# A transformer block with conditioning on one Trainium2 core: the start of the kernel reordered under a new table of operations

## The chip, the cores and the metric

The kernel runs on one core of a Trainium2 chip. The metric is device time in microseconds (us) of one execution. The core has five engines that run their own streams of instructions and meet at semaphores: TensorE (PE; its weight loads are shown as PEld), VectorE (DVE), ScalarE (ACT), GpSimd (POOL) and SyncE (SP). SP only issues transfers here, ACT issues a few. All inputs are bf16.

## The reference

The input x has 2048 rows of 640. A conditioning vector c gives six vectors of 640: shift, scale and gate for attention, and the same for the MLP. Heads are 32 of 20 columns; a row sees itself and the 255 rows before it.

```
mod = silu(c) @ w_mod                                    # 640 -> 6 x 640: sa, ca, ga, sb, cb, gb
h = layernorm(x) * (1 + ca) + sa
q, k, v = split(h @ wqkv)                                # 32 heads of 20
p = softmax(mask(q @ k.T * 20 ** -0.5))                  # 0 <= i - j < 256
x = x + ga * ((p @ v) @ wo)
h = layernorm(x) * (1 + cb) + sb
out = x + gb * ((sigmoid(h @ w_gate) * (h @ w_up)) @ w_down)   # inner width 1536
```

## The kernel before, in words

**Tiling.** The rows are cut into eight chunks of 256 (two blocks of 128). For each chunk: layer norm (`ln1`), projections to q, k and v (`qkv`), attention in two bursts of four head groups (`attention`), output projection (`outproj`), second layer norm, and the MLP (`mlp`). Chunks overlap: the projections of chunks two ahead and the MLP of an earlier chunk fill PE while ACT does the exponentials of attention.

**How the order is made.** The code records operations (`Prog.op`: engine, function, planned duration, what it reads and writes), and `Prog.schedule` goes through the long list `PLAN` (line 353). Each number is 5 times the number of an operation plus that of its engine (0 PE, 1 ACT, 2 DVE, 3 POOL, 4 SP); the list therefore fixes the order on every engine, and which engine does an operation that several can do. `schedule` also computes planned times from the planned durations, the planned landing of each DMA (`dlat` and work in us) and instruction fetches (`FETCH`), with least start times (`tmin`). They decide which buffer of a pool a tile gets; `emit` writes the instructions and the semaphore waits, and there is no waiting for a time on the chip. An engine does its instructions in this order: one that waits holds all behind it. The list itself was found by a search outside the file that uses the planned durations.

**The start.** SP issues x's block 0, then five tiles of w_mod for shift and scale of attention (320 KB each, into the buffer of w_down, hence the name `wd`), then halves of wq and wk with blocks 2 and 3 of x between them, then wv. ACT issues c and x's block 1. On the engines:

- The conditioning chain. A product with the identity turns c into a column (line 644, PE); DVE halves it (`c_col`, line 646); ACT takes tanh (line 647); DVE makes SiLU (`siluc`, line 648) and copies it to 64 columns (`silubc`, line 651, by DVE or ACT as PLAN says). Then ten products for each of the five tiles of w_mod (`fnA`, line 679 with `S<-silubc,wd`), and DVE copies the result to `mA` (line 759).
- The norm of chunk 0, block by block (`ln_stats`): two statistics of 320 columns each and an aggregate on DVE (lines 774 and 776); an addition and a power on POOL (lines 781 and 783), which give the reciprocal deviation; the normalisation on DVE (line 796). Five products with the identity transpose a block (`pe_transposes`, `M<-ident,x`), ACT and DVE empty the banks (lines 895 and 896), and `modulate` applies scale and shift to 128x128 pieces (lines 812 and 813). The projections need these pieces and wq.
- Warm-up products. DVE zeroes a strip of the buffer `E`; six operations `warm` (line 660) multiply it, five with two products of 512 columns and one with one, 11 in all. `fill` (line 671) adds single such products: one after each conditioning tile but the last, and two after the first block's transposes, where PLAN puts them. Their results aren't used.

**Later.** Queries and keys of chunks 0 and 1 are transposed on PE; from chunk 2 on, the normalised rows (`hT`), queries and keys (`QT`, `KT`, from the four buffers `stg`) and the input of the MLP (`h2T`) are transposed by DMA (`transp_dma`, line 803), issued on SP among all other transfers. The gate vectors are written to memory (`gate<-grow`) and read back for all partitions (`gbc<-gate`); DVE, or POOL, multiplies wo and w_down by them (lines 1316 and 1253). w_down, w_gate and w_up come in parts of 384 to 576 KB over the first 85 us. Results of PE go to four banks (`M`) and one large tile (`S`, scores). A bank is free again when DVE or ACT has emptied it.

**Edge sets.** In each of 14 half-chunks beyond the first, `edge_set` makes 64 products of 64x64 (line 680, `S<-QT,KT 20*64`) for the corners of the window; its planned duration is 0.36 us before.

Of the kernel before, what the change touches and what calls it, by code (L numbers as in the profile page):

```python
# [348 lines left out]
def c_pe(n):  # L349
# [147 lines left out]
def build(nc, A_x, A_wqkv, A_wo, B_x, B_w_gate, B_w_up, B_w_down, c, w_mod, out, S=2048):  # L497
    NCH = S // CH
    P = Prog(nc)
    A = P.op  # L500
# [32 lines left out]
    p_x1 = sbpool("x1", 6, [128, D])  # L533
# [23 lines left out]
    def R(name):  # L557
        return Res(name)
# [104 lines left out]
    for i in range(6):  # L663
        o = A("pe", warm if i < 5 else lambda e, g: warm(e, g, 1), 1.03 if i < 5 else 0.52, prio=90, reads=[R_z], extra=wprev, tag="warm", writes=[R("w")])
        wprev = [o]
# [705 lines left out]
```

## Time and profile before

| what | us |
|---|---|
| median of 3 runs (326.62 to 328.47) | 326.9 |
| the profiled execution | 330.35 |
| its span, first to last instruction | 328.6 |
| first projection product on PE | 12.76 |
| PE busy | 320.4 |

A row of the profile names the line, the engine, the operation, and output and inputs by the program's names; `xN` counts instructions. In a timeline the first two numbers are start and length in us. Matmuls are pipelined, so the length of a group holds the drain of its last product; the time to the next group's start is what the group costs. A row of waits reads: engine, output and line that waited `<-` who ended the wait: us in total, times, longest. DMA rows of the chain give the issue and the time until the landing that something waited for. The granted clock is a share of PE's full clock.

### The profile page before, as it was taken

How to read it: one execution, taken by the hardware profiler on the slowest of the kernel's cores; microseconds unless marked ns; L12 is line 12 of the kernel's file. 1: busy time of each engine (PE TensorE's matmuls, PEld its weight loads, DVE VectorE, ACT ScalarE, POOL GpSimd, SP SyncE). 2: the span in 40 equal slices, each digit the busy share in tenths (PEclk: the TensorE clock that was granted, in tenths of full speed). 3: DMA queues.
4: the chain of work that ended last, by engine and by line, in shares of the span. 5: the costliest groups of instructions: out<-in, count | busy, mean ns of one | idle time of the engine just before them, and what ended most of it. 6: DMA issues, size and time to landing. Idle time of an engine off the chain costs nothing.

```text
span 328.6 us, 11961 instructions
## 1 busy us (share of the span) xinstructions
PE 320.4 (97%) x5045; PEld 239.7 (73%) x5045; DVE 204.5 (62%) x421; ACT 212.8 (65%) x229; POOL 187.6 (57%) x325
## 2 busy tenths in 40 slices
PE   5999999989999999999999999999999999999996
PEld 2666766666777777776777778777888777887885
DVE  4589878549776666874476637463846366745422
ACT  1589999586977667877586767585686667220220
POOL 3148777564967767867675665748572859201000
PEclk9899999999999999999999999999999999999999
DMA  7996989999763562424553211374030213122201
GB/s 246 372 323 167 308 167 218 161 150 349 207 92 70 115 142 67 94 63 108 128 77 60 56 25 28 61 119 119 16 90 19 65 42 77 28 60 41 82 0 42
DMA packets 73007, 38.20 MB, mean 116 GB/s; under 512 B 46586, under 2 KB 71674, under 8 KB 72954
## 3 DMA queue, kind: packets, MB, share of 16 engines
q1 hardware_dynamic: 71936, 36.29, 46.7%
q10 hardware_dynamic: 1018, 1.15, 1.1%
q8 instruction: 40, 0.66, 0.8%
q14 instruction: 13, 0.11, 0.1%
HBM read 21.30 MB, written 5.25 MB: 81 GB/s over the span
## 4 chain that ended last, share of the span: by engine, by line
PE 89%; DMA 7%; DVE 2%; issue 1%; ACT 1%; SPq 0%; ACTq 0%; DVEq 0%
PE M L679 73%; PE S L680 8%; PE M L680 6%; DMA QT<-stg 2%; DMA hT<-x 2%; DMA gbc<-gate 2%; DMA x<-in_A_x_dram 1%; PE S L679 1%; ACT E L1016 1%; PE S L671 1%; SPq L803 0%; DVE V L896 0%; DVE wd L1253 0%; DVE st L774 0%; DVE T L1136 0%
## 5 line engine op out<-in xcount | busy, mean ns | idle before, releaser
L1051 POOL TENSOR_SCALAR_AFFINE_SELECT E<-E 128x512 bf16<-128x512 bf16 x224 | 141.8, 664 | 63.7 <-PE S L680 23.5
L1042 ACT ACTIVATE E<-S 128x2048 bf16<-128x2048 f32 x56 | 105.0, 1875 | 35.4 <-PE S L680 34.2
L679 PE MATMUL M<-h2T,wu 128*128 128x256 bf16 x480 | 70.5, 273 | 0.5 <-DVE T L1136 0.5
L679 PE MATMUL M<-h2T,wg 128*128 128x256 bf16 x480 | 65.6, 273 | 0.0
L679 PE MATMUL M<-wd,hh 128*128 128x320 bf16 (+2 forms) x396 | 56.9, 295 | 0.0
L679 PEld LDWEIGHTS M<-h2T,wu 128*128 128x128 bf16 x480 | 44.8, 98 | 9.1 <-DVE T L1136 0.8
L679 PEld LDWEIGHTS M<-h2T,wg 128*128 128x128 bf16 x480 | 46.0, 98 | 6.7
L1270 ACT ACTIVATE sig<-M 128x512 f32<-128x512 f32 x48 | 28.2, 596 | 32.1 <-PE M L679 31.0
L1272 DVE SCALAR_TENSOR_TENSOR hh<-sig,M 128x512 bf16<-128x512 f32 x48 | 32.2, 678 | 26.6 <-ACT sig L1270 17.4
L679 PEld LDWEIGHTS M<-wd,hh 128*128 128x128 bf16 x396 | 37.3, 98 | 14.0
L1291 DVE TENSOR_TENSOR x<-M,x 128x320 bf16<-128x320 f32 (+2 forms) x33 | 15.5, 480 | 35.4 <-PE M L679 35.1
L680 PE MATMUL S<-QT,KT 20*64 20x64 bf16 (+4 forms) x1856 | 34.9, 211 | 0.1
L680 PEld LDWEIGHTS S<-QT,KT 20*128 20x128 bf16 (+1 forms) x1856 | 22.1, 98 | 17.6 <-issue 9.2
L1016 ACT ACTIVATE E<-S 128x2048 bf16<-128x2048 f32 x14 | 26.3, 1877 | 10.2 <-PE S L680 10.2
L774 DVE BATCH_NORM_STATS2 st<-x 128x6 f32<-128x320 bf16 x64 | 28.6, 478 | 3.5 <-DMA x<-in_A_x_dram 3.2
L1136 DVE STREAM_TRANSPOSE T<-M 128x512 f32<-128x512 f32 x32 | 21.6, 700 | 14.5 <-PE S L680 13.5
L679 PE MATMUL M<-wk,hT 128*128 128x320 bf16 x160 | 26.6, 299 | 1.1 <-DVE V L896 1.1
L679 PE MATMUL M<-wq,hT 128*128 128x320 bf16 x160 | 26.9, 299 | 0.6 <-DMA QT<-stg 0.5
L679 PE MATMUL M<-wv,hT 128*128 128x320 bf16 x160 | 27.2, 300 | 0.0
L679 PE MATMUL M<-wo,oT 128*128 128x320 bf16 x160 | 25.4, 299 | 0.0
L680 PE MATMUL M<-E,V 128*32 128x256 bf16 (+1 forms) x960 | 23.0, 246 | 0.1
L680 PEld LDWEIGHTS M<-E,V 128*32 128x32 bf16 x960 | 19.1, 97 | 4.3 <-issue 2.7
(82 smaller groups left out, 321.5 us busy)
## 6 DMA issues: line engine op xcount, KB each, us to landing
x<-in_A_x_dram SPq DMA_DIRECT2D x23, 160.0 KB, 3.7
doc<-On SPq DMA_DIRECT2D x64, 40.0 KB
wd<-in_w_mod_dram SPq DMA_DIRECT2D x6, 320.0 KB
wd<-in_B_w_down_dram SPq DMA_DIRECT2D x4, 480.0 KB
out_dram<-x SPq DMA_DIRECT2D x11, 160.0 KB, 2.1
wu<-in_w_mod_dram SPq DMA_DIRECT2D x5, 320.0 KB, 6.7
oT<-doc SPq DMA_DIRECT2D x8, 192.0 KB, 2.7
wg<-in_B_w_gate_dram SPq DMA_DIRECT2D x2, 576.0 KB
```

What stands on the lines that cost most here:

```text
L671: ins = e.matmul(p_S.aps[0][:, 3, :], Eall[:, 0:128], Eall[:, 128:640], start=True, stop=True)
L679: return e.matmul(o, l, r, start=st, stop=sp, skip_group_check=True)
L680: return e.matmul(o, l, r, start=st, stop=sp, tile_position=tp, skip_group_check=True)
L774: A("dve", lambda e, g, bi=bi, j=j: e.bn_stats(v(bi * 12 + j * 6, 6), src[bi].ap[:, j * 320:(j + 1) * 320]), 0.48, reads=[src[bi].r()], wr ...
L1016: A("act", lambda e, eng: e.activation(G.ap[:], Sp.ap[:], ACT.Exp, scale=SM_SCALE), 1.876, reads=[Sp.r()], writes=[G.r()], prio=3, tag=f"e ...
L1042: A("act", lambda e, eng: e.activation(wide()[:, :, 64:320], Sp.ap[:].rearrange("p j (t c) -> p (j t) c", c=256), ACT.Exp, scale=SM_SCALE) ...
L1051: A("pool", lambda e, eng, ap=ap, inp=inp, pat=pat, base=base, cm=cm: e.affine_select(ap(), inp(), pattern=pat, compare_op=ALU.is_ge, fill ...
L1136: A("dve", lambda e, g, h=h: e.transpose(T1.ap[:, 512 * h:512 * h + 512], X[h].ap), 0.694, reads=[X[h].r()], writes=[T1.r(h)], prio=3.5, t ...
L1270: A("act", lambda e, g, pg=pg, sg=sg: e.activation(sg.ap[:], pg.ap[:], ACT.Tanh, scale=0.5), c_act(512), reads=[pg.r()], writes=[sg.r()], ...
L1272: A("dve", lambda e, g, pu=pu, sg=sg, f0=f0: e.scalar_tensor_tensor(out=hh.ap[:, f0:f0 + 2, :], in0=sg.ap[:].rearrange("p (a b) -> p a b", ...
L1291: A("dve", lambda e, g, ps=ps, bi=bi, c0=c0, n=n: e.tensor_tensor(x1[bi].ap[:, c0:c0 + n], ps.ap[:, 0:n], x1[bi].ap[:, c0:c0 + n], op=ALU. ...
```

## The change

The table PLAN is new throughout, and so is the order on all engines. Beside it:

- Nine warm-up operations (17 products) instead of six (11). In the new table they stand thus on PE: two products, the start of the conditioning sum, two products, the product for c, ten products, transposes of block 0, two conditioning tiles, three products, the third tile, transposes of block 1, the last two tiles, and then all six fills. Before, transposes of block 0, two tiles, two fills, transposes of block 1, three tiles, four fills.
- DVE now does `c_col` between the two statistics of block 0, then aggregate, `siluc` and the normalisation of block 0, and then the statistics of block 1. Before: statistics of block 0, `c_col`, aggregate, statistics and aggregate of block 1, `siluc`, `silubc`, normalisation of block 0. `silubc` is on ACT now. Two memsets of `stg` moved from POOL to the start of DVE.
- SP issues both halves of wq one after the other (before, block 2 of x stood between them). Around 45 to 80 us, before: a part of w_down, QT, KT, KT, QT, hT, a part of w_down, hT, QT, KT, QT, KT, gbc, h2T twice. Now: QT, KT, the gate, a part of w_down, QT, KT, gbc, hT, hT, QT, a part of w_down, KT, QT, KT, h2T twice.
- The modulation of that hT, three pieces on ACT and two on DVE, is now four on ACT and one on POOL. Other evacuations and modulations of chunks 2 to 7 also moved between ACT, DVE and POOL.
- Planned figures: landing of x's block 1 (4.6 instead of 2.95 us) and of the first w_mod tiles (4.0 instead of 2.89), least start of the projections' weights 2.4, an instruction fetch left out, warm-up lengths, and 0.54 instead of 0.36 us for an edge set.

```diff
@@ -473 +474 @@ FETCH
-    4.30, 15.19, 23.69, 31.86, 36.07, 43.09, 49.13, 56.81, 65.53, 72.11, 81.79, 85.91, 94.33, 102.58, 109.61, 119.26,
+    -5, 15.19, 23.69, 31.86, 36.07, 43.09, 49.13, 56.81, 65.53, 72.11, 81.79, 85.91, 94.33, 102.58, 109.61, 119.26,
@@ load_x
-            dlat=2.95 if pool is p_x1 and b < 4 else 2.24)
+            dlat=(2.95, 4.6, 2.95, 2.95)[b] if pool is p_x1 and b < 4 else 2.24)
@@ load_w3
-                    (2.2 if hi - lo == 640 else 1.12), writes=[R_w3[k][lo // 320]] if halves else R_w3[k], prio=prio, tag=k)
+                    (2.2 if hi - lo == 640 else 1.12), writes=[R_w3[k][lo // 320]] if halves else R_w3[k], prio=prio, tag=k,
+                tmin=2.4)
...
-    load_bulk(wm_ap[0], wm_src[:, :, 0:1280], Rm[0], 0.88, 0.2, "wm0", dlat=2.89)
+    load_bulk(wm_ap[0], wm_src[:, :, 0:1280], Rm[0], 0.88, 0.2, "wm0", dlat=4.0)
@@ warm
-    for i in range(6):
-        o = A("pe", warm if i < 5 else lambda e, g: warm(e, g, 1), 1.03 if i < 5 else 0.52, prio=90, reads=[R_z], extra=wprev, tag="warm", writes=[R("w")])
+    for i in range(9):
+        o = A("pe", warm if i < 8 else lambda e, g: warm(e, g, 1), 1.03 if i < 3 else 0.6 if i < 8 else 0.3, prio=90, reads=[R_z], extra=wprev, tag="warm", writes=[R("w")])
@@ edge_set
-        last["s"] = [with_pv(f"edge{a}", sc, 0.36, rd, [G, Sp], before, 3)]
+        last["s"] = [with_pv(f"edge{a}", sc, 0.54, rd, [G, Sp], before, 3)]
```

225 rows, old and new, of the table PLAN are left out of this document.

## The prediction

> **What bounds the kernel now.** I read the page first, then who waited for whom on TensorE (PE), the busy time by stretch, and the order of time on DVE and PE in the head.
>
> ```profile
> span 328.6 us, 11961 instructions
> ## 1 busy us (share of the span) xinstructions
> PE 320.4 (97%) x5045; PEld 239.7 (73%) x5045; DVE 204.5 (62%) x421; ACT 212.8 (65%) x229; POOL 187.6 (57%) x325
> ```
> ```profile
> PE M L679 <- DVE x L796: 2.1, 1, 2.1
> PE S L660 <- DVE E L655: 1.3, 1, 1.3
> PE M L679 <- DVE V L896: 1.1, 1, 1.1
> PE M L679 <- DMA QT<-stg: 0.5, 1, 0.5
> PE M L679 <- DVE T L1136: 0.5, 1, 0.5
> ```
> ```profile
> 4.20:7.61 3.41, 1.35 (x6) 0.39 (x4) 2.12 (x8) 0.21 (x1) 1.04 (x3) 1.00 1.00 359
> 7.61:11.02 3.41, 3.36 (x40) 2.81 (x41) 0.80 (x3) 0.86 (x2) 1.00 (x2) 0.51 1.09 357
> 0.00:8.05 8.05, 4.63 (x17) 1.75 (x18) 3.63 (x12) 1.49 (x2) 3.09 (x18) 0.98 0.73 244
> 22.00:36.00 14.00, 14.00 (x278) 9.86 (x275) 13.66 (x35) 13.14 (x16) 9.82 (x13) 1.00 0.75 222
> 80.00:320.00 240.00, 240.00 (x3838) 185.19 (x3838) 142.85 (x276) 153.52 (x150) 140.67 (x232) 1.00 0.35 77
> ```
>
> PE is idle for 8.2 us in all (328.6 minus 320.4). Five waits hold 5.5 us of it: two in the head (1.3 at the very start, 2.1 before the first transposes of x) and three, 2.1 us together, between 50 and 80 us. The stretches give, after their length, busy time on PE, weight loads, DVE, ACT and POOL, then the granted clock, the DMA share and GB/s. From 80 to 320 us PE is busy 240.00 of 240 us: there a new order can lose time, hardly win any. The head is worse than its idle time shows: PE worked 1.35 of the 3.41 us to 7.61, and the granted clock of the next 3.41 us was 0.51.
>
> ```profile
> 3.21 0.89 DVE L774 BATCH_NORM_STATS2 st<-x 128x6 f32<-128x320 bf16 x2 [1.97 <-DMA x<-in_A_x_dram]
> 4.02 0.15 DVE L646 TENSOR_SCALAR c_col<-M 128x5 bf16<-128x5 f32 x1
> 4.13 0.21 DVE L776 BATCH_NORM_AGGREGATE st<-st 128x2 f32<-128x12 f32 x1
> 5.57 0.89 DVE L774 BATCH_NORM_STATS2 st<-x 128x6 f32<-128x320 bf16 x2 [1.22 <-DMA x<-in_A_x_dram]
> 6.49 0.21 DVE L776 BATCH_NORM_AGGREGATE st<-st 128x2 f32<-128x12 f32 x1
> 6.62 0.11 DVE L648 SCALAR_TENSOR_TENSOR siluc<-cth,c_col 128x5 bf16<-128x5 f32 x1
> 6.76 0.49 DVE L651 COPY silubc<-siluc 128x320 bf16<-128x320 bf16 x1
> 7.17 0.44 DVE L796 TENSOR_SCALAR x<-x,st 128x640 bf16<-128x640 bf16 x1
> ```
> ```profile
> 3.48 2.07 PE L660 MATMUL S<-E 128*128 128x512 bf16 x7
> 7.66 0.71 PE L679 MATMUL M<-ident,x 128*128 128x128 bf16 x5 [2.11 <-DVE x L796]
> 8.17 1.27 PE L679 MATMUL S<-silubc,wd 128*128 128x64 bf16 x20
> 9.25 1.04 PE L671 MATMUL S<-E 128*128 128x512 bf16 x2
> 10.09 0.74 PE L679 MATMUL M<-ident,x 128*128 128x128 bf16 x5
> 10.62 1.26 PE L679 MATMUL S<-silubc,wd 128*128 128x64 bf16 x30
> 11.71 1.03 PE L671 MATMUL S<-E 128*128 128x512 bf16 x4
> 12.76 1.74 PE L679 MATMUL M<-wq,hT 128*128 128x320 bf16 x10
> ```
>
> These are starts and lengths, in order of time. DVE waits until 5.57 for x1's transfer (1.22 us), and behind x1's statistics stand SiLU of c, its broadcast, and the normalisation of x0 (x̂0 here). So x0, in the core since 3.21, reaches PE at 7.66; then the conditioning products run partly at half clock, and the first projection starts at 12.76. From there PE is dense but for the three waits.
>
> **The change, part by part: the head.** On DVE the changed order is: half of x0's statistics, c_col, the other half, aggregate, SiLU, x̂0, and only then x1's statistics. The broadcast goes to ACT.
>
> ```profile
> 4.43 0.24 POOL L781 TENSOR_SCALAR st<-st 128x1 f32<-128x1 f32 x1 [2.05 <-DVE st L776]
> 4.75 0.58 POOL L783 TENSOR_TENSOR st<-st,mhalf 128x1 f32<-128x1 f32 x1
> ```
> ```profile
> 1.24 2.31 SPq L574 DMA_DIRECT2D wd<-in_w_mod_dram  x5
> ```
> ```profile
> wu<-in_w_mod_dram SPq DMA_DIRECT2D x5, 320.0 KB, 6.7
> ```
>
> *x̂0:* 3.21 + 0.89 + 0.15 + 0.21 ends the aggregate near 4.45; POOL's add and power (0.24 + 0.58 and 0.1 between) end near 5.4; x̂0 takes 0.44 and is ready at 5.85, not 7.61. Tanh, SiLU and broadcast lie beside POOL's power. The broadcast on ACT isn't in the trace: between 0 and twice DVE's 0.49, I take 0.49; it would have to last past 6.5 to delay a product, so it costs nothing.
>
> *Warm-ups:* nine operations are 17 products instead of 11. One takes 0.42 at half clock (9.25 to 10.09 for two), so 0.21 at full. Ten instead of seven stand behind the c product; they start at 3.48 as now, and with three more the last one ends its turn near 5.9 to 6.1. That holds x0's transposes by 0.2 us at most, and x1 is still to come: nothing on the path. In exchange PE has no gap there, and three more fill the time between the conditioning tiles.
>
> *x1:* DVE is free at 5.85, so its statistics begin 0.3 later than 5.57 and end at 6.95 (0.89 + 0.21). Add and power, 7.9; a memset and an evacuation on DVE fit in that time. x̂1 is done at 8.4, its transposes start near 8.5 instead of 10.09 and take 0.27 (half of 10.09 to 10.62).
>
> *What is late next* is w_mod. c, x0, x1 and five tiles of 320 KB are 1.97 MB, and 244 GB/s over 8.05 us is that amount: the last byte moves at 8.05. The last tile was issued near 3.1; by the median 6.7 us to landing of the same tiles of the next part it lands at 9.8. Between 8.05 and 9.8 I take 9.35, nearer to the row that includes the landing. Its ten products take 0.27 at full clock (20 took 1.08 at half): done at 9.65. Six fills now follow instead of four, 6 x 0.21 = 1.26, and the projections start at 10.95. From the last product to the first projection now pass 1.05 us (11.71 to 12.76) with copy and modulation in them; the fills cover that. So 12.76 becomes 10.95: **-1.8 us**. wq's second half goes ahead of x2 now; 400 KB at 359 GB/s are 1.1 us, so wq lands near 10.5 and 11.6, and the second is needed 0.7 after 10.95: just in time. Bounds: -2.3 if w_mod lands with x̂1, near 8.8; -0.9 at half clock (third rival).
>
> [...]
>
> **The change: 45 to 80 us.** The new table also moves DMAs in SP's queue and shares of work between DVE, ACT and POOL. The arithmetic stays, and so does the number of changes of tile mode on PE (159 in both orders).
>
> ```profile
> 49.33 7.33 DMA QT<-stg
> 56.79 2.85 PE M L679 x20
> 59.64 6.33 DMA hT<-x
> 67.77 1.23 SPq L803
> 69.10 5.02 DMA gbc<-gate
> ```
> ```profile
> L574 SPq DMA_DIRECT2D gate<-grow x1: 632/632/632, 27.3 to 27.3; - x1
> L574 SPq DMA_DIRECT2D gbc<-gate x1: 1382/1382/1382, 33.0 to 33.0; - x1
> ```
>
> The chain of waits runs through three transfers here, and the three waits of PE hang on them. A part of w_down (480 KB) stands ahead of the first QT transpose (7.33 us from issue to landing) and the next between the two of hT (6.33); DVE modulates that hT in its order and only then empties V's banks (1.1 us on PE); gbc comes last, so the scaling of w_down holds the transposes of T (0.5). In the changed order the first QT and KT stand ahead of w_down, both hT ahead of its next part, DVE modulates no tile of that hT, and gbc is issued ahead of hT. Each cause is gone, but SP and the banks have as much to do, so something else may be late in its place. Between 0 and 2.1 us I take half: **-1.1 us**. The edge sets' length, the landing times and the least start times in the planner are figures for ordering; no instruction gets longer by them: 0. In the tail the last product (192 columns), its addition and the last store stand in the same order: 0.
>
> Sum: 330.35 (the profiled execution; its span is 328.6) - 1.8 - 1.1 = 327.45. The median of the runs is 3.45 lower, 326.9; I carry the 2.9 us over: **324.0**.
>
> **Rivals.**
> *The middle gives nothing* (waits of the same size in other places): only the head counts, 325.1. For it: an order this full leaves little room, PE is already busy 14.00 of 14 us at 22 to 36. Against: each of the three waits has a cause that the order takes away.
> *The head is used up.* From 22 to 36 us DVE is busy 13.66 and ACT 13.14 of 14 us. If they set the pace there, the earlier start ends in waits: all of 1.8 is lost, 326.9 with nothing in the middle. Against it: PE has 14.00 of 14, and their work starts earlier too.
> *Half clock again.* One execution shows how the clock's stretches lie to the kernel's start. If the one with x1's transposes and the fills is half, five transposes, ten products for each of two tiles and two fills take 0.53 + 1.08 + 0.84 from 8.5 on, to 11.0, then four fills 0.84: 11.8, -0.9 for the head, 324.9 with the middle.
> *SP held: slower.* gbc now stands ahead of hT and waits for the gate's write. The first gate was issued at 27.3, and its gbc's issue ended at 34.4, so that write took up to 7 us; beside transposes it may take QT's 7.33. The w_down part, QT and KT between them cover about 3.1 (0.6 and twice 1.23). Then SP stands 4.2 us with hT behind it, and PE has no other projections: -1.8 + 4.2, 329.3. It decides from a write of 4.9 us on (no gain left); slower by over 0.5% from 6.5.
>
> **How the numbers follow.** 0.5%, 1.6 us, is about what a measurement can tell from no change, so faster is below 325.3. Chances: forecast 0.46, middle nothing 0.22, head used up 0.11, half clock 0.08, SP held 0.13. Of these faster: 0.42, 0.12, 0, 0.06, 0, together 0.60; slower 0.13; same the rest, 0.27. The range goes from 322.0 (2.3 and 2.1 from 326.9, and 0.5 of scatter) to 328.3, halfway to the slower rival from the third case; it leaves that rival out.
>
> **What would show it.** Right: PE without a gap from 1.3 to 7 us, granted clock 1.00 from 7.6 to 11, first wq product near 11.0, no waits for V, QT and T. Wrong: a first wq product after 12, a clock near 0.5 there, gbc's issue on SP lasting several us, or idle time on PE beyond 80 us.

## The result and the profile after

The changed kernel is slower: 331.75 us median of 4 runs (331.14 to 333.11) against 326.98 for before beside it (4 runs, 326.62 to 328.47). The ratio on record is 1.0115, interval 1.0066 to 1.0164 (the quotient of the two medians is 1.0146, inside it). The forecast was 324.0, the range 322.0 to 328.3. The profiled execution of after took 331.14 us.

The page, and who waited for whom on PE (engine, output, line `<-` releaser: us, times, longest), both of after:

```profile
span 329.4 us, 11959 instructions
PE 321.6 (98%) x5051; PEld 239.3 (73%) x5051; DVE 206.9 (63%) x427; ACT 212.6 (65%) x224; POOL 189.2 (57%) x324
```
```profile
PE M L681 <- DMA KT<-stg: 1.3, 2, 0.8
PE S L662 <- DVE E L657: 1.3, 1, 1.3
PE M L681 <- DVE st L776: 1.0, 1, 1.0
PE M L682 <- ACT E L1018: 0.7, 1, 0.7
PE M L681 <- POOL hT L823: 0.5, 1, 0.5
PE M L681 <- DMA QT<-stg: 0.2, 1, 0.2
```

The wait for x̂0 in the head is gone, and so are the waits for V and T. Six others stand there (KT's line holds two), five of them between 50 and 72 us; the sixth, for POOL's hT, ends at 148.75. The head of after on PE (start, length):

```profile
3.50 4.28 PE L662 MATMUL S<-E 128*128 128x512 bf16 x10
7.62 0.44 PE L681 MATMUL M<-ident,x 128*128 128x128 bf16 x5
...
11.77 2.43 PE L681 MATMUL M<-wq,hT 128*128 128x320 bf16 x16
```
```profile
5.44 0.45 DVE L798 TENSOR_SCALAR x<-x,st 128x640 bf16<-128x640 bf16 x1 [1.00 <-POOL st L785]
```

x̂0 is ready at 5.89 (5.44 + 0.45), as forecast, but its transposes start at 7.62: ten warm-up products stand ahead of them and take 4.12 us from start to start, 0.41 each. The first projection starts at 11.77, 1.0 us earlier than in the profile of before.

That profile of before was the first thing to doubt. Its execution took 330.35 us with a median of 326.9. Another execution of the unchanged kernel (e1 below) took 326.44 us, and its trace reads otherwise:

```profile
span 324.7 us, 11960 instructions
```
```profile
PE S L660 <- DVE E L655: 1.3, 1, 1.3
PE M L679 <- DVE x L796: 0.7, 1, 0.7
PE M L679 <- ACT hT L820: 0.7, 1, 0.7
```
```profile
3.48 3.19 PE L660 MATMUL S<-E 128*128 128x512 bf16 x7
7.41 0.45 PE L679 MATMUL M<-ident,x 128*128 128x128 bf16 x5 [0.73 <-DVE x L796]
10.91 1.74 PE L679 MATMUL M<-wq,hT 128*128 128x320 bf16 x10
```

Here before starts its projections at 10.91, not 12.76; the wait for x̂0 is 0.7, not 2.1; and the waits for V, QT and T, which were to be won, don't exist. So after is to be compared with this trace. Busy time by stretch (length, then busy PE, weight loads, DVE, ACT, POOL; granted clock, DMA share, GB/s), first after, then e1:

```profile
36.00:60.00 24.00, 22.07 (x429) 14.70 (x426) 19.77 (x43) 21.21 (x24) 19.05 (x34) 1.00 1.00 208
60.00:80.00 20.00, 18.63 (x291) 13.16 (x292) 12.42 (x28) 14.09 (x22) 12.06 (x20) 1.00 1.03 229
80.00:160.00 80.00, 79.39 (x1365) 58.83 (x1363) 53.67 (x109) 60.15 (x60) 60.36 (x99) 1.00 0.50 106
```
```profile
36.00:60.00 24.00, 23.20 (x436) 16.03 (x435) 19.34 (x43) 20.30 (x28) 18.51 (x33) 1.00 0.95 212
60.00:80.00 20.00, 20.00 (x334) 14.73 (x327) 15.38 (x30) 16.43 (x21) 11.81 (x20) 1.00 1.02 251
80.00:160.00 80.00, 79.99 (x1421) 59.48 (x1419) 51.93 (x109) 58.76 (x59) 60.94 (x102) 1.00 0.52 106
```

After's PE loses 1.13 us more between 36 and 60 (23.20 - 22.07), 1.37 between 60 and 80, and 0.60 between 80 and 160, where before loses nothing. The same instruction in both, products of E and V, serves as a milestone; first after, then e1:

```profile
73.56 1.50 PE L682 MATMUL M<-E,V 128*32 128x256 bf16 x64
...
161.66 1.50 PE L682 MATMUL M<-E,V 128*32 128x256 bf16 x64
```
```profile
69.82 1.59 PE L680 MATMUL M<-E,V 128*32 128x256 bf16 x64
...
157.27 1.50 PE L680 MATMUL M<-E,V 128*32 128x256 bf16 x64
```

After is 0.86 us late at the first projection, 3.74 at 70 us, 3.66 at 140 (143.68 against 140.02), 4.39 at 157, and 4.7 at the end (329.4 - 324.7). What is lost stands between the head and 74 us (2.9) and from 140 us on (1.0). The chain of waits of after shows where the first part is lost (the end of that stretch stands here); SP's issues (start, length) of after and of e1 stand below it, with w_down's part:

```profile
67.36 4.61 DMA KT<-stg
72.11 1.52 PE M L681 x10
```
```profile
61.45 1.24 SPq L805 DMA_TRANSPOSE QT<-stg  x1
62.73 0.58 SPq L575 DMA_DIRECT2D wd<-in_B_w_down_dram  x1
...
64.84 2.42 SPq L805 DMA_TRANSPOSE QT<-stg  x1
67.36 1.25 SPq L805 DMA_TRANSPOSE KT<-stg  x1
```
```profile
59.87 1.23 SPq L803 DMA_TRANSPOSE QT<-stg  x1
...
64.04 1.24 SPq L803 DMA_TRANSPOSE KT<-stg  x1
```

The last KT transpose of chunk 3 is issued 3.3 us later than in before, lands at 71.97 (67.36 + 4.61), and PE's next products start at 72.11. In e1's chain no transfer stands between 48 and 80 us.

### The profile page after: what moved, and what is told of

Same layout as the page of the kernel before. It is cut to its first block, busy times and chain, and to the rows that moved or that the text cites. A ratio compares the mean times of both kernels' runs of the same rounds, so it can differ in the third digit from the quotient of the medians.

```text
span 329.4 us, 11959 instructions
## 1 busy us (share of the span) xinstructions
PE 321.6 (98%) x5051; PEld 239.3 (73%) x5051; DVE 206.9 (63%) x427; ACT 212.6 (65%) x224; POOL 189.2 (57%) x324
## 4 chain that ended last, share of the span: by engine, by line
PE 94%; DMA 3%; DVE 1%; ACT 1%; POOL 1%; issue 0%
PE M L681 75%; PE S L682 9%; PE M L682 7%; PE S L662 2%; DMA QT<-stg 2%; DMA KT<-stg 1%; ACT E L1018 1%; PE S L681 1%; DVE T L1138 0%; PE S L673 0%; POOL hT L823 0%; DVE st L776 0%; POOL E L1053 0%; DVE stg L898 0%; DVE x L1293 0%
## 5 line engine op out<-in xcount | busy, mean ns | idle before, releaser
L681 PE MATMUL M<-h2T,wu 128*128 128x256 bf16 x480 | 68.3, 273 | 0.0
L681 PE MATMUL M<-h2T,wg 128*128 128x256 bf16 x480 | 66.6, 273 | 0.0
L1274 DVE SCALAR_TENSOR_TENSOR hh<-sig,M 128x512 bf16<-128x512 f32 x48 | 32.0, 674 | 30.4 <-ACT sig L1272 19.9
L681 PE MATMUL M<-wk,hT 128*128 128x320 bf16 x160 | 27.6, 299 | 0.7 <-DMA KT<-stg 0.5
L898 DVE CAST stg<-M 128x320 bf16<-128x320 f32 x35 | 16.7, 483 | 13.8 <-PE M L681 13.7
```

Source lines behind the costliest of these rows:

```text
L681: return e.matmul(o, l, r, start=st, stop=sp, skip_group_check=True)
L898: return e.tensor_copy(dst(), src())
L1274: A("dve", lambda e, g, pu=pu, sg=sg, f0=f0: e.scalar_tensor_tensor(out=hh.ap[:, f0:f0 + 2, :], in0=sg.ap[:].rearrange("p (a b) -> p a b", ...
```

## The experiments

Two theories. **A:** the profile of before showed an untypical execution; the waits that the change was to remove are mostly not there in others, and the new order brings waits of its own. **B:** the profile was typical, and the new order alone destroys a real gain. Orders in the diffs are those of PLAN; times are medians beside runs of before on the same chip.

**e1, before again.**

> The kernel before, unchanged, for a second profile. Theory A (the profile of before was an unusual execution: a half-clock stretch from 7.6 to 11.0 us and the three waits behind it cost it the 3.4 us by which it lies over its median): about 327 us, span near 325, first wq product before 12, and fewer or shorter waits between 45 and 80 us. Theory B (the profiling itself adds the 3.4 us): the profile again shows a span near 328.6 and the first wq product at 12.7, whatever the timed runs give.

326.83 us, ratio 0.998 (0.9952 to 1.0008); profiled execution 326.44, first projection 10.91. A holds. Over the five batches of runs below, before was run 121 times, 325.45 to 330.88 us, and 4 of these took 330 us or more. The mean granted clock tells more: in the profile of before it was 0.995, which is what its one stretch of 3.41 us at half clock makes of the whole (1.7 of 328.6 us lost). Only 8 of the 121 runs had 0.995; their median is 329.5, that of the other 113 is 327.35. So such executions are rare and some 2.2 us longer. Where the clock fell in the eight isn't on record, and not every long run is of this kind: the longest, 330.88, had 1.000.

**e2, e3, e4, e5: the head and the rest apart.**

```diff
 e2  conditioning, blocks 0 and 1: order of after (nine warm-ups); all else: order of before
 e3  conditioning, blocks 0 and 1: order of before (six warm-ups); all else: order of after
 e4  order of before
+    three more warm-ups behind the sixth
 e5  as e2
-    nine warm-ups
+    six warm-ups
```

e2, e3 and e5 have the planned figures of after, e4 those of before.

> The changed order for the start alone (warm-ups, conditioning chain, norm of chunk 0, memsets, up to the modulation of chunk 0), and the order of before for all that follows. Theory A (what comes after 13 us in the new table costs the 4.8 us; the head is a gain or nothing): 325.5 to 327. Rival C (the new head itself costs, by nine warm-ups at half clock that hold the transposes): 329 to 332, like the whole change.

> The order of before for the start with six warm-ups, and the order of the changed kernel for all that follows. Theory A: 331 to 333, the loss of the whole change or a little more. Rival C: about 327, as before.

> The kernel before with three more warm-up operations (17 products instead of 11) right behind the others, all else as before. Theory A: within 1 us of before; they fill a gap of PE and at most hold the transposes of x0 by some 0.5 us if the clock is half there. Rival C: 1 us or more over before, since at half clock ten products of 0.42 end at 7.7 and hold the transposes.

> The changed head with six warm-up operations instead of nine, and before's order for all the rest. Theory (the three added operations, ten products in a row at half clock, are what makes the changed head late: 11.79 us for the first wq product in the run with nine and the old rest, 10.91 in the run of before): first wq product at 10.9 to 11.2, median 326.9 to 327.6. Rival (the order itself, x1's statistics behind x0's normalisation and all fills last, makes it late): 11.6 or later, and 328.3 as with nine.

| | median us | ratio, interval | first wq product |
|---|---|---|---|
| e2 new head, old rest | 328.34 | 1.0026 (1.0001 to 1.0051) | 11.79 |
| e3 old head, new rest | 330.87 | 1.0108 (1.0063 to 1.0154) | 11.20 |
| e4 before, nine warm-ups | 327.70 | 1.0001 (0.9977 to 1.0026) | 10.68 |
| e5 new head, six warm-ups, old rest | 327.24 | 1.0000 (0.9977 to 1.0022) | 11.14 |

The rest of the table carries nearly the whole loss (e3); the new head gives nothing, with nine warm-ups perhaps a little less than nothing (e2's 328.34 lies between the two cases expected for it). Warm-ups by themselves cost nothing (e4), and neither do after's planned figures: e5 has them, but for the warm-ups' lengths, and stands at 1.0000. That nine instead of six make e2 slower than e5 is likely by the medians, but the intervals overlap, and the two profiled executions differ in their clock as well (the row of ten warm-ups is 4.30 us long in e2, 0.41 from one start to the next; that of seven is 2.26 in e5).

**e9, after again.**

> The changed kernel, unaltered, beside the next three on one chip and with another profiled execution. Theory (the profiled execution of before was one where the clock rose early; the changed head depends on the same thing, 10.8 us to the first wq product where the ten warm-ups end at full clock, 11.8 where all ten ran at half): median 331.2 to 332.0 as before; first wq product near 10.8 or near 11.8, and the end with it. Rival (the head is slow for another reason, the clock has no part): a first wq product near 11.8 though warm-ups ran at full clock.

330.92 us, ratio 1.0116 (1.0083 to 1.0148). Its head and its waits:

```profile
3.50 3.20 PE L662 MATMUL S<-E 128*128 128x512 bf16 x10
6.55 0.44 PE L681 MATMUL M<-ident,x 128*128 128x128 bf16 x5
10.98 2.57 PE L681 MATMUL M<-wq,hT 128*128 128x320 bf16 x17
73.74 1.50 PE L682 MATMUL M<-E,V 128*32 128x256 bf16 x64
```
```profile
PE M L681 <- DMA KT<-stg: 1.9, 2, 1.1
PE M L681 <- DVE x L1227: 1.1, 1, 1.1
PE M L681 <- DMA QT<-stg: 0.8, 1, 0.8
```

The same ten warm-ups take 3.05 us here: the first four at half clock (0.40 to 0.43 from start to start), the last five at full (0.216). The first projection starts at 10.98, 0.8 earlier than in the other execution of the same kernel, and at the milestone of 73.6 nothing is left of it (73.74 against 73.56): the waits for KT and QT have grown by 1.2 (2.7 against 1.5). So in these two executions the clock decides how late the new head is, and the transposes make it no matter. Over all nine profiles with the new head and nine warm-ups (after, e2, e7 to e11, e15, e17) the first projection starts at 10.81 to 11.81.

**e8, e10, e17: parts of the new order undone between 45 and 75 us.**

```diff
 e8  SP of after, from 50 us
-    KT, gate, w_down, QT, KT, gbc, hT, hT, QT, w_down, KT, QT, KT, h2T, h2T
+    KT, gate, QT, KT, w_down, gbc, hT, hT, QT, KT, QT, KT, h2T, h2T, w_down
 e10 ACT of after, from 47 us; DVE, from 58 us
-    two modulations of hT, exponential of the edge set | evacuation, statistics, evacuation
+    exponential of the edge set, two modulations of hT | evacuation, evacuation, statistics
 e17 SP of after
-    gbc, hT, hT, QT, w_down, KT, QT, KT, h2T
+    hT, hT, QT, w_down, KT, QT, KT, gbc, h2T
```

> The changed kernel with two parts of w_down (issued on SP at 52.5 and 62.7 us) moved behind the transposes that follow them: the first behind KT at 55.5, the second behind h2T at 68.7. Theory (bulk ahead of a transpose makes KT late; PE's two waits for KT, 1.3 us, and some 0.4 of QT's end with it): 330.0 to 330.5. Rival (the transposes are late because their source tiles come late, SP stands before them anyway): 331.5 to 332, the waits for KT as long as now.

> The changed kernel with two swaps in the orders by hand: on ACT the exponential of the edge set (48.90 us) ahead of two modulations of hT, on DVE one evacuation to stg (59.05) ahead of one statistics instruction. Theory (these two hold PE at 49.9 for 0.86 and at 58.7 for 0.44 of 1.18 us): up to 1.3 less, 330.4 to 331.2, and no wait for E of line 1018. Rival (the wait only moves, since KT comes late anyway): within 0.4 of the changed kernel.

> The changed kernel with gbc behind the transposes of chunk 3. If gbc's place makes them late, they are issued 1 us earlier and the median falls by 0.5 to 1.5, to 329.5 to 330.5; if it doesn't, within 0.4 of the changed kernel (330.9 to 331.8 so far).

e8: 330.23 us, 1.0083 (1.0052 to 1.0114). The last KT of chunk 3 is issued at 64.19 instead of 67.36, the second part of w_down behind the transposes at 69.12, and the waits for KT and QT are gone. The milestone stands at 70.12, where e1 has 69.82 and e9 73.74; but PE then waits 1.0 us for a part of w_gate:

```profile
64.19 1.27 SPq L805 DMA_TRANSPOSE KT<-stg  x1
69.12 0.57 SPq L575 DMA_DIRECT2D wd<-in_B_w_down_dram  x1
```
```profile
70.12 1.50 PE L682 MATMUL M<-E,V 128*32 128x256 bf16 x64
```
```profile
PE M L681 <- DMA wg<-in_B_w_gate_dram: 1.0, 1, 1.0
```

Its head (10.81) was only 0.17 earlier than e9's, so nearly all of the 3.6 us between these two milestones comes from w_down's place. e13 below, with the same move, has 70.38; the eight other profiles with after's order at that place and w_down among the transposes (after, e3, e7, e9, e10, e11, e15, e17) have 72.18 to 74.49. The next products of E and V start at 88.52 in e8, again 1.4 behind e1's 87.15, about the wait for w_gate. By the medians the edit is worth 0.7 to 1.5 us (330.23 against 330.92 and 331.75), the intervals of e8 and after overlap, and the profiled execution of e8 (329.02) was its fastest.

e10: 331.82 us, 1.0149 (1.0117 to 1.0182): the wait for E is gone, that for a statistics instruction is now one for stg (0.6), both waits for KT are still there, and nothing was gained. The rival had it within 0.4 of the changed kernel; it is 0.9 above e9 and level with the first 331.75.

e17: 332.89 us, 1.0165 (1.0118 to 1.0212), slower by 1 to 2 us, which neither case had. Its chain and DVE say why:

```profile
PE M L682 <- DVE stg L898: 3.3, 1, 3.3
```
```profile
67.05 3.93 DMA gbc<-gate
```
```profile
71.07 0.49 DVE L1255 TENSOR_TENSOR wd<-wd,gbc 128x640 bf16<-128x640 bf16 x1 [4.10 <-DMA gbc<-gate]
73.50 1.25 DVE L898 CAST stg<-M 128x320 bf16<-128x320 f32 x3
```

In the new order DVE scales w_down ahead of three evacuations. With gbc issued at 67.05, DVE stands 4.1 us, the evacuations stand behind it, and PE stands for them. The place of gbc on SP and of the scaling on DVE belong together. What gbc's early place costs the transposes e17 can't tell by its time: the last KT is issued at 65.71, 1.3 to 1.7 us earlier than in e9 and after, and PE's waits for KT and QT are gone, but DVE's stand covers it.

**e14, e16, e18: single parts of the new order put into before.**

```diff
 e14, e18  SP of before, from 47 us
-    w_down, QT, KT, KT, QT, hT, w_down, hT, QT, KT, QT, KT, gbc
+    QT, KT, KT, w_down, QT, hT, hT, QT, w_down, KT, QT, KT, gbc
 e16 SP of before
-    hT, w_down, hT, QT, KT, QT, KT, gbc
+    gbc, hT, w_down, hT, QT, KT, QT, KT
```

> Before with one thing of the change: its two parts of w_down stand where the changed order has them, the first ahead of the last QT transpose of chunk 2, the second between QT and KT of chunk 3. Theory (a transpose issued behind w_down holds SP for 2.4 instead of 1.25 us, and KT of chunk 3 comes late): 0.6 to 1.5 us over before. Rival (before has slack there; w_down's place costs only together with sources that come late): within 0.5 us of before.

> Before with one thing of the change: the read of the gate (gbc) ahead of the two hT transposes. Rival of the prediction (SP stands there until the gate's write lands): gbc's issue lasts over 2 us and the median is 1 us or more over before. Theory (the write, issued 8 us before, has landed; gbc takes SP about 0.5 us): within 0.5 us of before.

> Before with its two parts of w_down ahead of the last QT transpose of chunk 2 and between QT and KT of chunk 3, once more. If the gain was real (the two hT transposes stand together, and what waited for hT in the longer executions of before waits no more): 0.994 to 0.999 of before and again little scatter, below 1.5 us from least to most, where before has 4 to 5. If it was the luck of a batch: 0.999 to 1.002.

e14: 326.21 us, 0.9964 (0.9944 to 0.9984); e18, the same kernel in another batch: 326.52 us, 0.9966 (0.9939 to 0.9993). This is **faster than both kernels**, by little: both intervals end below 1, but the unchanged kernel of e1 also came out at 0.998 against its neighbours. The theory that w_down's place by itself makes the transposes late has fallen: in before's order the new place costs nothing and gains some 0.3%. SP of e14:

```profile
53.79 2.96 SPq L803 DMA_TRANSPOSE hT<-x  x2
57.22 1.53 SPq L803 DMA_TRANSPOSE QT<-stg  x1
63.43 1.23 SPq L803 DMA_TRANSPOSE KT<-stg  x1
```

Both hT are issued by 56.8 (in e1 by 59.3: 57.66 + 1.66), and of PE's waits only those of the head are left (in e18 also 0.3 for an hT and 0.4 at 42 us). From the products of E and V near 50 us to the next near 70 pass 19.7 us in e14 and 19.9 in e18. Where w_down has before's place it is 20.4 to 21.6 in six profiles (before, e1, e2, e4, e5, e16) and 19.6 in one (e6): the new place avoids a wait of half a microsecond or more that most executions of the old one have. The runs went from 325.33 to 327.17 and from 325.95 to 328.16, before beside them from 325.8 to 330.9. That is not the scatter below 1.5 us that was expected, and e1's ten runs of before lay within 1.3 us, so less scatter isn't shown. None of these 24 runs had the granted clock of 0.995 that 8 of the 121 of before had, which by that share chance alone may give.

e16: 326.95 us, 0.9987 (0.9962 to 1.0012); gbc takes 0.49 us on SP at 55.83. The gate's write doesn't hold SP.

**e6, e7, e15, e11: the late part.**

```diff
 e6  order of before for what it plans ahead of 80 us, then order of after
 e7  order of after ahead of 81 us, then order of before
 e15 order of after ahead of 138 us, then order of before
 e11 order of after; two pieces of chunk 7's modulation of hT
-    POOL
+    DVE
```

> Before's order for what it plans ahead of 80 us, the changed order behind that. Theory (the changed table loses some time also behind 80 us, where before has PE busy without a gap): 0.8 to 1.6 us over before, 328.0 to 328.8. Rival (all is lost between 45 and 80 us): 327.0 to 327.5.

> The changed order up to 81 us of the plan, before's order behind that. Theory (head 0.9 and 45 to 80 us 2.3 late, against the run of before): 330.0 to 330.8. Rival (the late part carries most of the loss): 328.5 or less.

> The changed order up to 138 us, before's order behind. Theory (behind 81 us all is lost from 140 us on, where modulations of hT on POOL stand behind masks): as with the join at 81 us, 329.0 to 330.0. Rival (the loss lies between 81 and 138 us, or each join costs): 330.7 or more.

> The changed kernel with the two pieces of chunk 7's modulation that it has on POOL (146 to 149 us) on DVE. Theory (wv's products wait for POOL there, 0.6 us with nothing behind it to make up): no wait for POOL's hT, 0.6 less, 331.0 to 331.3. Rival (the products wait for something else then): within 0.2 of the changed kernel.

e7: 329.50 us, 1.0062 (1.0037 to 1.0088); e15: 329.54 us, 1.0069 (1.0039 to 1.0099). Both joins gain the same 1.4 us against e9, though on other chips and with intervals that overlap e9's. That speaks for a late loss behind 138 us alone, and the traces of after and e1 agree: level from 74 to 140 us, 1.0 lost behind.

e6: 332.36 us, 1.0151 (1.0103 to 1.0199), slower than after: at its join PE waits 2.0 us for a mask on POOL, a cost of the join, so its time tells nothing of the late part. Its trace does: from the products of E and V at 143.60 to the next at 161.60 pass 18.0 us, as in after (143.68 to 161.66), where e1 takes 17.25 (140.02 to 157.27). So the late order loses this by itself, whatever stands ahead of it.

e11: 331.14 us, 1.0123 (1.0089 to 1.0157), a miss: the time lies in the theory's 331.0 to 331.3, but beside e9 (330.92) nothing is gained. The wait for POOL's hT is gone, and another of the same size stands 13 us later, in front of the next products of E and V:

```profile
162.21 1.50 PE L682 MATMUL M<-E,V 128*32 128x256 bf16 x64 [0.68 <-DVE x L1227]
```

**e12, e13: the repairs together.**

```diff
 e12 order of after ahead of 81 us with six warm-ups, the edits of e8 and e10; then order of before
 e13 as e12
-    the edits of e10
```

> The changed order up to 81 us with six warm-up operations, both parts of w_down behind the transposes and the two swaps of the run before; before's order behind 81 us. Theory (the losses are separate orders that add up: from the run with the changed order up to 81 us, 329.5, off 1.5 for w_down, about 1.0 for the warm-ups and up to 1.2 for the swaps): 325.8 to 327.2, before or a little less. Rival (the changed order packs projections so closely that each repair only shows the next wait): 328.5 or more.

> The repaired version without the two swaps: changed order up to 81 us with six warm-up operations and both parts of w_down behind the transposes, before's order behind. Theory (w_down and the late part are the losses; the swaps gave nothing and may cost up to 0.9): 327.0 to 327.9, before's time, not below it. Rival (the head's gain comes through once the transposes are on time): 325.5 to 326.5.

e12: 327.87 us, 1.0029 (0.9998 to 1.0060), between its two cases; e13: 328.50 us, 1.0041 (1.0012 to 1.0070), above both of its own. Most of the loss comes back (after stands at 1.0115), but nothing of a gain appears: in e13's trace (a long execution, 330.9 us) PE waits 2.4 us for w_gate, as it did in e8 for 1.0. With w_down behind the transposes the next transfer is late, though not in e12's trace. Whether the two swaps help here can't be told (the intervals overlap).

## Why the prediction was wrong, point by point

**The sum against the profiled execution, carried over to the median: this is the step that failed.** The text saw that the profile lay 3.45 us above the median and moved the sum down by that much, as if an overhead. It was a part of the waits themselves. In e1 the first projection starts 1.85 us earlier than in the profile of before, and by 70 us PE is 3.0 ahead (69.82 against 72.84). The 1.8 and 1.1 that were forecast as gains are of just this size (1.85 in the head, 1.2 behind it), and they were counted twice: once in the lower median and once as won. Without them the sum's own logic says no gain. That is 2.9 of the 7.75 us between 324.0 and 331.75; the other 4.85 are losses, for which the sum left no room. By the traces of after and e1 they are 0.9 in the head, 2.9 between the head and 74 us and 1.0 behind 140 us.

**Head, -1.8.** The mechanism was sized well where the warm-ups ended at full clock: 10.98 in e9 for 10.95 forecast. But the base was wrong. In seven other profiles with before's head (e1, e3, e4, e6, e14, e16, e18; e4 with nine warm-ups) the first projection starts at 10.68 to 11.37; 12.76 was the exception. Against 10.91 the new head is level in e9 and 0.86 late in the profile of after. The sub-step that failed with it is the end of the warm-ups at 5.9 to 6.1: the ten took 4.12 us in one execution and 3.05 in another, since the clock rose later in both (between 7.3 and 7.6 us, and near 5.3) than in the profile of before (4.3). That clock is the third rival's subject, but in another place: not the fills ran at half (after's six take 1.46 us in all, four took 1.03 in before), the warm-ups did (0.41 a product in after).

**45 to 80 us, -1.1.** Each of the three waits named is gone, but in e1 they were not there to remove; in other executions with before's order some are, and shorter in sum (0.7 for V and 0.4 for QT in e16, 0.9 for T in e4). The first rival (waits of the same size in other places) came nearest, and it was too mild: they are larger, 2.9 us later at the milestone. So the step's range, from 0 to 2.1 us of gain, left out what happened: a loss. The cost stands where chunk 3's transposes are issued, up to 3.3 us later. In the new order it is w_down's place among them: with both parts behind, the milestone is back at 70.12 (e8) and 70.38 (e13). In before's order the same place costs nothing (e14). The medians give back only 0.7 to 1.5 us; in the traces of e8 and e13 a wait for w_gate takes some of it back. gbc's place costs nothing in before's order (e16); what it costs in the new one stays open (e17), and so does why w_down's place costs in one order and not in the other. The swaps on ACT and DVE (e10) give nothing back.

One piece of that step was right: with w_down away from the two hT, and behind the first QT and KT, a wait goes out of before. Done alone, with the rest of before's order kept, these two moves are worth some 0.3% (e14, e18); which of them, wasn't taken apart.

**Beyond 80 us, nothing.** The text says that a new order can lose time there, and then puts it at 0. It lost 1.0 in the traces, between 144 and 178 us; in which instructions wasn't found (e11 only moved the wait).

**SP held, slower.** The sign came true, the mechanism didn't: gbc's issue takes 0.45 us in after, 0.50 in e9 and 0.49 in e16, not 4.2 (1.53 is the most, in e8). **Edge sets' and other planned figures** were put at 0, and that holds by e5, which has them (without the warm-ups' lengths) and stands at 1.0000. **The head used up** is what e9 shows, though not through DVE and ACT at 22 to 36 us, but through the transposes before 74 us. **The range's upper end** is given as halfway from 326.9 to 329.3, which is 328.1 and not 328.3; the result lies far above either.

## What to carry to other kernels

Before a wait is priced, ask whether the profiled execution is a typical one: where it lies above the median, the excess may sit in the very waits that a change takes away, as here, and then nothing is gained on the median. Here a second execution of the unchanged kernel and the granted clock of the runs told. Where several engines and queues follow orders that were written together, a new order for all of them is judged by what stands *behind* each moved instruction; here single repairs mostly showed the next wait. Two moves in the old order (both parts of w_down) were worth more than the whole new table.

## What the runs showed of the hardware

The rise of PE's clock at the start wandered from one execution to the next. By the step from 0.427 to 0.216 us between 512-column products it came at 4.3 us in the profile of before, near 5.3 in e9, after 6.0 in e1 and between 7.3 and 7.6 in after, with products running since 1.30 in all of them: 3.0 to over 6.0 us later. What sets the point, no run shows.

The granted clock doesn't show this start. The stretch from 4.20 to 7.61 us in after and in e9:

```profile
4.20:7.61 3.41, 3.41 (x9) 1.21 (x8) 1.90 (x7) 0.47 (x1) 1.53 (x6) 1.00 1.00 352
```
```profile
4.20:7.61 3.41, 3.41 (x35) 1.90 (x34) 2.17 (x8) 0.96 (x2) 1.53 (x6) 1.00 0.97 345
```

Both read 1.00 and fully busy, but after's PE did 9 products in it, 0.427 us from one to the next, while e9's warm-ups went over to 0.216 within it. The count tells it, or the time from one product to the next.

Later the granted clock does show a fall, and the length of an idle gap alone doesn't foretell it. PE's longest wait was 2.1 us in the profile of before, 2.4 in e13 and 3.3 in e17. In before the 3.41 us behind that wait have a granted clock of 0.51; over the whole execution the mean was 0.995 in before and in e13, and 1.000 in e17. What decides it, no run shows.
